# Product of q and decay moved to VectorE, narrowing steps spread evenly, first unit reordered with its constants filled by GpSimd

## The chip, the cores and the metric

The kernel runs on one core of a Trainium2 chip. Five engines work from queues of their own: TensorE (PE, with its weight loads PEld), VectorE (DVE), ScalarE (ACT), GpSimd (POOL) and SyncE (SP, which here only issues transfers). The metric is the device time of one execution in microseconds; the kernel before takes 841.13 us, the median of 3 runs (839.98 to 841.34).

## The reference

Three stages follow one another. Inputs are float32, but the weights of the third stage (`moe2_w_in`, `moe2_w_out`) are float64 and reach the chip as pairs of 32-bit words.

```
f = 1/(1+exp(-f_logit))                        # 4 batches, 8 heads, 768 steps, 48 wide
for t: state = f[t][:,None]*state + outer(k[t],v[t]);  y[t] = q[t] @ state
x = y as (3072, 384);  logits = x @ w_gate     # 8 experts, each takes exactly 384 tokens,
                                               # handed out greedily by logit
x[mask_e] = relu(x[mask_e] @ w1[e]) @ w2[e]
h = x @ w_in;  out = (h*clip(h+3,0,6)/6) @ w_out
```

## The kernel before, in words

`attention` computes the first stage and the logits. The time axis is cut into 24 chunks of 128 steps (index `j`), and two chunks make a unit of 256 steps (12 units, index `u`). All heads are done together. For each unit f, k and q are loaded as pairs of neighbouring steps. `decay` makes ft = (tanh(f/2)) and then 0.5*x+0.5 on ScalarE (L76, L77), and the product of each pair of decays on VectorE into `pmf` (L78). `queries` multiplies the even q by the decay (L85, GpSimd) and copies the odd q (L86, ScalarE). `keys` does the same for k (L81 VectorE, L82 ScalarE). TensorE then transposes: `decays` (L91, ScalarE copies the result to `ff`, L94), `turned` for q and k (L112). VectorE runs a scan for prefix products (`prefix`, L98), a reciprocal (`ends`, L100), a reversed scan (`suffix`, L106), and scales the transposed q and k by them (`scaled`, L125, to `qt` and `kh`). `kept` (L103) stores the decay of a chunk.

For each chunk `ya_mm` issues the state matmuls (L151) and the scores of the next chunk (L145), interleaved; `a_ev` copies the scores out (L177, ScalarE) and masks them (L178, GpSimd); `y_mm` multiplies by v (L202) and ScalarE copies the result to `yt` (L203 or L204); `kt_mm` transposes `kh` (L185, L186); `kv_mm` makes the state's increment (L213), which VectorE adds (L220) and GpSimd scales (L221); `l_mm` gives x and the logits (L227, L229, L232). PSUM tiles named `pT` rotate through five banks, so a transpose may have to wait until an earlier tile of the rotation has been read.

The order is written out by hand in the loop over `j`. With `ti=0` (odd `j`) the unit after the current one is started: `tg(0)` to `tg(3)` call `slot` with n=0 to 3, and with `ti=1` (even `j`) with n=4 to 7. `slot` issues that slot's transposes and its VectorE operations (table `OPS`), and puts a "fill" behind the first of them (or behind the deferred operations of `late`, where the slot has none).

The fill, `take(i)`, advances the generator `prep` by `PREP[ti][i]` steps, and `END[ti]` more are taken at the end of a chunk: the narrowing of the float64 weights. A block of 512 columns takes three steps: (a) ScalarE's rounding copy (L720) and GpSimd's remainder (L721) of the block before, and VectorE's first operation on this block (L923); (b) VectorE L925; (c) VectorE L927, and the transfer (L933) that refills the freed buffer, of which there are two. Blocks of `w_out` (L958, L963 in place of L720, L721) take four. Before, the steps are taken as follows:

```
PREP=((2,0,1,0),(0,0,2,0)); END=(0,1)
```

That is three per chunk up to j=19, then two per slot until none are left. In this order step (c) and the next step (a) fall into the same fill: L720 of a block stands on ScalarE's queue right behind VectorE's L927 of that block.

Ahead of the loop, constants are filled on VectorE (L27 to L59), SyncE issues f, k, q of unit 0 in halves of four heads and then v and the gate's weights (L235 to L239), and the loop at L246 prepares unit 0, one half wholly after the other. Behind the attention come the routing and eight experts.

Of the kernel before, what the change touches and what calls it, by code (L numbers as in the profile page):

```python
# [10 lines left out]
F32=mybir.dt.float32; F32R=mybir.dt.float32r; BF=mybir.dt.bfloat16; I32=mybir.dt.int32; U32=mybir.dt.uint32  # L11
AF=mybir.ActivationFunctionType; OP=mybir.AluOpType; AX=mybir.AxisListType
PS=bass.MemoryType.PSUM
B,H,S,D=4,8,768,48
C=128; U=256; G=C//2; NP=4; NU=B*S//U; NCH=B*S//C
PMIN=2.0**-60; PB=5

def attention(tc, q,k,v,f,wg, x_dram, lg, ident, pmin, ranges, prep, setup, spin):
    nc=tc.nc
    ctx=ExitStack()  # L20
    with ctx:
        ld=ctx.enter_context(tc.tile_pool(name="ald",bufs=2))
        cs=ctx.enter_context(tc.tile_pool(name="acs",bufs=1))
# [4 lines left out]
        for nm in 'kq':  # L28
            t=cs.tile([128,2,NP,2,64],F32,name=f"pm{nm}")
# [3 lines left out]
        ft=cs.tile([128,2,H,D],F32,name="ft")  # L33
        L=G+1; W2=4*L
        held=ps.tile([128,512],F32,name="pC"); m0=held[:,:W2-1]; m1=held[:,512-W2:]
        nc.vector.memset(held,0.0)
        for n in range(4):
            nc.vector.memset(held[:,n*L+G-1:n*L+G],PMIN)
            if n: nc.vector.memset(held[:,n*L-1:n*L],1.0)
        PXB=[]  # L40
        for i in range(2):
            t=cs.tile([128,NP,2,L],F32,name=f"P{i}"); nc.vector.memset(t,1.0); PXB.append(t)
        SW=cs.tile([128,NP,2*D+8],F32,name="sw"); nc.vector.memset(SW,0.0)
        for s in range(2):
            for o in range(2):
                b=(s^o)*D
                nc.vector.tensor_copy(SW[64*s:64*s+48,o::2,b:b+D],ident[64*s:64*s+48,None,64*s:64*s+D].to_broadcast([48,NP//2,D]))
        VP=[]
        for i in range(2):
            t=cs.tile([128,2,H,64],F32,name=f"v{i}"); nc.gpsimd.memset(t[:,:,:,D:],0.0); VP.append(t)  # L50
        KHB=[]
        for i in range(2):
            t=cs.tile([128,NP,U],F32,name=f"kh{i}"); KHB.append(t)
        St=[]
        for i in range(2):
            t=cs.tile([128,NP,64],F32,name=f"St{i}"); nc.vector.memset(t[:,:,D:],0.0); St.append(t)
        FF=[]
        for i in range(2):
            t=cs.tile([128,W2+4],F32,name=f"ff{i}"); nc.vector.memset(t,0.0); FF.append(t)  # L59
        raw={}  # L60
        def load(u,nm,h0=0,h1=H):
            b,o=divmod(u*U,S)
            if nm!='v':
                src={'f':f,'k':k,'q':q}[nm]
                t=ld.tile([128,H,2*D],F32,name=nm+"r",bufs=1) if h0==0 else raw[nm,u]
                nc.sync.dma_start(t[:,h0:h1],bass.AP(tensor=src.tensor,offset=src.offset+b*H*S*D+h0*S*D+o*D,ap=[[2*D,128],[S*D,h1-h0],[1,2*D]]))
            else:
                t=VP[u%2]
                for c in range(2):
                    nc.sync.dma_start(t[:,c,:,:D],bass.AP(tensor=v.tensor,offset=v.offset+b*H*S*D+(o+c*C)*D,ap=[[D,C],[S*D,H],[1,D]]))  # L70
            raw[nm,u]=t
        view=lambda u,nm: raw[nm,u].rearrange("p h (r d) -> p r h d",d=D)
        home=lambda nm,r: perm[nm][:,r].rearrange("p a s d -> p (a s) d")[:,:,:48]
        def decay(u,i,h0=0,h1=H):
            x=ft[:,:,h0:h1]
            if i==0: nc.scalar.activation(x,view(u,'f')[:,:,h0:h1],AF.Tanh,scale=0.5)  # L76
            elif i==1: nc.scalar.activation(x,x,AF.Identity,bias=half[:,0:1],scale=0.5)  # L77
            else: nc.vector.tensor_mul(perm['f'].rearrange("p a s d -> p (a s) d")[:,h0:h1,:48],ft[:,0,h0:h1],ft[:,1,h0:h1])  # L78
        def keys(u,i,h0=0,h1=H):
            x=view(u,'k')[:,:,h0:h1]  # L80
            if i==0: nc.vector.tensor_mul(home('k',0)[:,h0:h1],x[:,0],ft[:,1,h0:h1])  # L81
            else: nc.scalar.copy(home('k',1)[:,h0:h1],x[:,1])  # L82
        def queries(u,i,h0=0,h1=H):
            x=view(u,'q')[:,:,h0:h1]
            if i==0: nc.gpsimd.tensor_tensor(out=home('q',0)[:,h0:h1],in0=x[:,0],in1=ft[:,0,h0:h1],op=OP.mult)  # L85
            else: nc.scalar.copy(home('q',1)[:,h0:h1],x[:,1])  # L86
        KH={};QT={};PC={};PX={};SX={}
        V=nc.vector
        def decays(u,pairs):
            pt=ps.tile([128,512],F32,name="pT",bufs=PB).rearrange("p (a c g) -> p a c g",a=NP,c=2)  # L90
            for p in pairs: nc.tensor.transpose(pt[:,p].rearrange("p c g -> p (c g)"),perm['f'][:,p].rearrange("p a d -> p (a d)"),ident)  # L91
            for h in sorted({p//2 for p in pairs}):
                ff=FF[h][:,:W2].rearrange("p (a c g) -> p a c g",a=2,c=2)
                nc.scalar.copy(ff[:,:,:,1:],pt[:,2*h:2*h+2])  # L94
        flat=lambda t: t.rearrange("p a c g -> p (a c g)")
        def prefix(u,h):
            PX[u]=PXB[u%2]
            V.tensor_tensor_scan(flat(PX[u][:,2*h:2*h+2])[:,1:],FF[h][:,1:W2],m0,1.0,op0=OP.mult,op1=OP.max)  # L98
        def ends(u,h):
            V.reciprocal(m1.rearrange("p (a c g) -> p a c g",a=2,c=2)[:,:,:,G],PX[u][:,2*h:2*h+2,:,G])  # L100
# [3 lines left out]
        def suffix(u,h):  # L104
            SX[u,h]=wk.tile([128,2,2,L],F32,name="S",bufs=2)
            V.tensor_tensor_scan(flat(SX[u,h])[:,1:][:,::-1],FF[h][:,2:W2+1][:,::-1],m1[:,1:][:,::-1],0.0,op0=OP.mult,op1=OP.max)  # L106
        PT={}
        def turned(u,nm,h):
            pt=ps.tile([128,512],F32,name="pT",bufs=PB).rearrange("p (a g r) -> p a g r",a=2,r=2)
            for a in range(2):  # L110
                for r in range(2):
                    nc.tensor.transpose(pt[:,a,:,r],perm[nm][:,r,2*h+a].rearrange("p s d -> p (s d)"),ident)  # L112
            PT[u,nm,h]=pt
        def scaled(u,nm,h):
            if nm=='k': o=KH[u]=KHB[u%2]
            elif h==0: o=QT[u]=wk.tile([128,NP,U],F32,name="qt")
            else: o=QT[u]
            pt=PT.pop((u,nm,h))
            x=SX[u,h] if nm=='k' else PX[u][:,2*h:2*h+2]
            x=x.rearrange("p a c g -> p (a c) g")  # L120
            i0=pt.rearrange("p a (c g) r -> p (a c) g r",c=2); out=o[:,2*h:2*h+2].rearrange("p a (c g r) -> p (a c) g r",c=2,r=2)
            if nm=='k': i1=x[:,:,1:][:,:,:,None].to_broadcast([128,4,G,2])
            else:
                i1=x[:,:,0:G]; i1=bass.AP(tensor=i1.tensor,offset=i1.offset,ap=list(i1.ap)+[[1,2]])
            V.tensor_tensor(out=out,in0=i0,in1=i1,op=OP.mult)  # L125
# [107 lines left out]
            later.append(lambda: nc.sync.dma_start(x_dram[j*C:(j+1)*C,:],y.rearrange("p a d -> p (a d)")))  # L233
        ranges=ranges(lambda: ps.tile([128,384],F32,name="pT",bufs=PB),lambda: ps.tile([128,512],F32,name="pT",bufs=PB))
        for h in (0,4):  # L235
            for nm in 'fkq': load(0,nm,h,h+4)
        load(0,'v')
        for s in range(2):
            for o in range(2): nc.sync.dma_start(SW[64*s:64*s+48,o::2,2*D:],wg.rearrange("(p s d) e -> s d p e",p=NP,s=2)[s^o][:,o::2])  # L239
# [1 line left out]
        def warm(n):  # L241

            t=ps.tile([128,512],F32,name="pT",bufs=PB)
            for _ in range(n): nc.tensor.matmul(t[:,:128],ident,ident,start=True,stop=True)
        warm(WARM[0])
        for h in range(2):  # L246
            hh=(4*h,4*h+4)
            for i in range(3): decay(0,i,*hh)
            for i in range(2): queries(0,i,*hh)
            decays(0,(2*h,2*h+1))  # L250
            for i in range(2): keys(0,i,*hh)
            prefix(0,h); ends(0,h)
            warm(WARM[1])
            turned(0,'q',h); suffix(0,h); scaled(0,'q',h)
            turned(0,'k',h); scaled(0,'k',h)
            warm(WARM[1+h])
        kept(0)
        for nm in 'fqk': load(1,nm)
        later=[]
# [7 lines left out]
        next(prep)  # L267
        while later: later.pop(0)()
        constants,early=setup()
        PREP=((2,0,1,0),(0,0,2,0)); END=(0,1)  # L270
        for j in range(-1,NCH+1):
            tu,ti=divmod(j+1,2)
            tu+=1
            if j>=0 and j%2==0 and j//2+1<NU: load(j//2+1,'v')
            def take(i):
                for _ in range(PREP[ti][i] if j<20 else 2): next(prep,None)
            def tg(i): slot(tu,4*ti+i,(lambda: take(i)) if j>=0 else None)
            if j==NCH: spin(lambda: ps.tile([128,384],F32,name="pT",bufs=PB),TAIL[0])
            tg(0)
            if 0<=j-1<NCH: l_mm(j-1)  # L280
            if j==NCH: spin(lambda: ps.tile([128,384],F32,name="pT",bufs=PB),TAIL[1])
            tg(1)
            while later: later.pop(0)()
            if 0<=j<NCH: y_mm(j,0)
            ya_mm(j)
            if j+1<NCH:
                a_ev(j+1,0)
                a_ev(j+1,1)
            if ti==1: refill(tu+1,'f',2)
            if 0<=j<NCH: y_mm(j,1)  # L290
            if j>=0: kv_mm(j)
            tg(2)
            if ti==0 and tu<NU: kept(tu)
            if ti==0: refill(tu+1,'f',0)
            if j+1<NCH: kt_mm(j+1)
            if ti==1:
                for i in range(2): refill(tu+1,'q',i)
            tg(3)
            if ti==0: refill(tu+1,'f',1)
            if ti==1:  # L300
                for i in range(2): refill(tu+1,'k',i)
            if j>=0: next(constants,None)
            if j>=NCH-4: next(ranges,None)
            if j in (17,22,24): next(early)
            if j<20:
                for _ in range(END[ti] if j>=0 else 0): next(prep,None)
# [843 lines left out]
```

## Time and profile before

| | |
|---|---|
| median of 3 runs | 841.13 us |
| the profiled execution's own time | 845.23 us |
| its span, first to last instruction | 843.2 us |
| PE busy | 793.5 us, 94% |
| PEld busy | 761.9 us, 90% |
| DVE busy | 549.6 us, 65% |
| ACT busy | 364.0 us, 43% |
| POOL busy | 134.7 us, 16% |
| mean granted TensorE clock | 0.982 |

Busy shares are means over stages with different limits. TensorE's row is modelled from pipelined matmuls, so 94% does not say that it runs at its peak. The attention ends, and the last chunk's L202 starts, at 166.62 us of the span; the experts' first matmul starts at 195.35 us.

### The profile page before, as it was taken

What the parts mean: (1) busy time and instruction counts of PE and PEld (TensorE: products, weight loads), DVE (VectorE), ACT (ScalarE), POOL (GpSimd) and SP (SyncE); (2) the same over time, 40 slices, a digit from 0 to 9 for tenths busy, and PEclk for the clock granted to TensorE, in tenths of its full rate; (3) what the DMA queues carried; (4) which work ended last, traced back from release to release, by engine and by line L of the source; (5) the groups of instructions that cost most, each with busy time, mean ns of one, the idle gap of its engine ahead of it and who ended that gap; (6) DMA issues with size and microseconds to landing.
All of it is one profiled execution on the core that took longest, in us unless ns stands there. A gap on an engine that the chain in (4) does not pass through costs nothing.

```text
span 843.2 us, 16692 instructions
## 1 busy us (share of the span) xinstructions
PE 793.5 (94%) x6387; PEld 761.9 (90%) x6387; DVE 549.6 (65%) x1522; ACT 364.0 (43%) x757; POOL 134.7 (16%) x215
## 2 busy tenths in 40 slices
PE   7887899978999999999999999999999999999994
PEld 6776788767989899899999999999999999999994
DVE  7898789777688647846875776667766523642431
ACT  4776677523244325423542454154316423541431
POOL 2665554211001100010101101100200020010001
PEclk9999899988999999999999999999999999999998
DMA  9898897272013112311422232322232321321000
GB/s 220 201 236 203 204 267 185 59 252 87 1 38 113 57 39 59 101 38 57 134 70 77 87 100 82 91 79 83 87 92 83 91 90 57 113 87 47 10 1 32
DMA packets 99032, 84.54 MB, mean 100 GB/s; under 512 B 67328, under 2 KB 86912, under 8 KB 98944
## 3 DMA queue, kind: packets, MB, share of 16 engines
q1 hardware_dynamic: 95872, 73.96, 31.5%
q0 software_dynamic: 3072, 9.44, 3.6%
q8 instruction: 52, 0.85, 0.4%
q14 instruction: 36, 0.29, 0.1%
HBM read 73.94 MB, written 9.44 MB: 99 GB/s over the span
## 4 chain that ended last, share of the span: by engine, by line
PE 57%; issue 10%; DVE 8%; ACT 2%; DMA 2%; POOL 1%; POOLq 0%; SPq 0%; DVEq 0%; ACTq 0%
PE pF L724 9%; PE acc L724 9%; PE pF L725 9%; PE pF L726 9%; PE acc L726 9%; PE acc L725 9%; DMA xg<-x_dram,q_ids 1%; DVE ga L867 1%; DVE hl L870 1%; ACT hh L869 1%; DVE w1l L773 1%; PE pF L811 1%; POOL out_dram L901 1%; DVE q_ge L502 1%; POOL xg L790 1%
## 5 line engine op out<-in xcount | busy, mean ns | idle before, releaser
L724 PE MATMUL acc<-wo,hh 128*128 128x384 f32 x384 | 134.0, 349 | 0.0
L724 PE MATMUL pF<-xh,wih 128*128 128x384 f32 x384 | 131.0, 341 | 0.0
L867 DVE SCALAR_TENSOR_TENSOR ga<-ga,pF 128x384 f32<-128x384 f32 x128 | 70.8, 553 | 92.3 <-ACT ga L866 92.0
L726 PE MATMUL acc<-wo,hh 128*128 128x384 f32 x384 | 129.7, 338 | 0.0
L725 PE MATMUL acc<-wo,hl 128*128 128x384 f32 x384 | 129.5, 337 | 0.0
L725 PE MATMUL pF<-xh,wil 128*128 128x384 f32 x384 | 129.4, 337 | 0.0
L726 PE MATMUL pF<-xl,wih 128*128 128x384 f32 x384 | 129.3, 337 | 0.0
L866 ACT ACTIVATE ga<-pF,three 128x384 f32<-128x384 f32 x128 | 74.1, 579 | 98.9 <-PE pF L726 92.1
L869 ACT CAST hh<-ga 128x384 fp32r<-128x384 f32 x128 | 65.8, 514 | 98.4 <-DVE ga L867 92.9
L870 DVE TENSOR_TENSOR hl<-ga,hh 128x384 fp32r<-128x384 f32 x128 | 71.2, 556 | 29.7 <-ACT hh L869 27.7
L832 ACT ACTIVATE hh<-pF 128x384 fp32r<-128x384 f32 x64 | 31.5, 492 | 132.4 <-PE pF L726 125.1
L901 POOL DMA_INDIRECT out_dram<-ga,q_ids x24 | 24.3, 1011 | 396.7 <-ACT ga L899 393.9
L833 DVE SCALAR_TENSOR_TENSOR hl<-pF,hh 128x384 fp32r<-128x384 f32 x64 | 35.6, 556 | 71.2 <-ACT hh L832 70.8
L724 PEld LDWEIGHTS acc<-wo,hh 128*128 128x128 f32 x384 | 72.5, 189 | 1.6 <-ACT ga L866 1.5
L725 PEld LDWEIGHTS acc<-wo,hl 128*128 128x128 f32 x384 | 72.5, 189 | 0.2 <-DVE hl L870 0.2
L726 PEld LDWEIGHTS acc<-wo,hh 128*128 128x128 f32 x384 | 72.4, 188 | 0.0
L724 PEld LDWEIGHTS pF<-xh,wih 128*128 128x128 f32 x384 | 72.2, 188 | 0.0
L725 PEld LDWEIGHTS pF<-xh,wil 128*128 128x128 f32 x384 | 72.2, 188 | 0.0
L726 PEld LDWEIGHTS pF<-xl,wih 128*128 128x128 f32 x384 | 72.1, 188 | 0.0
L724 PE MATMUL pF<-xh,w1h 128*128 128x384 f32 x192 | 66.8, 348 | 0.6 <-ACT xh L802 0.6
L724 PE MATMUL acc<-hh,w2h 128*128 128x384 f32 x192 | 65.9, 343 | 0.0
L726 PE MATMUL pF<-xl,w1h 128*128 128x384 f32 x192 | 64.9, 338 | 0.0
(285 smaller groups left out, 1623.5 us busy)
## 6 DMA issues: line engine op xcount, KB each, us to landing
wst<-in_moe_w_dram SPq DMA_DIRECT2D x58, 192.0 KB, 2.4
wst<-in_moe_w_dram SPq DMA_DIRECT2D x42, 256.0 KB, 3.0
pw<-in_moe_w_in_dram SPq DMA_DIRECT2D x12, 512.0 KB, 5.1
wo<-in_moe_w_out_dram SPq DMA_DIRECT2D x16, 384.0 KB, 4.3
pm<-in_moe_w_out_dram SPq DMA_DIRECT2D x32, 192.0 KB, 2.5
pm<-in_moe_w_in_dram SPq DMA_DIRECT2D x30, 192.0 KB, 2.6
v<-in_v_dram SPq DMA_DIRECT2D x24, 192.0 KB, 5.2
x_dram<-y SPq DMA_DIRECT2D x24, 192.0 KB, 4.9
```

The source lines that it names most:

```text
L502: V.scalar_tensor_tensor(ge[:,c0:c1],x[:,c0:c1,None].to_broadcast([128,c1-c0,32]),base[:,0:1],grid[:,None,:].to_broadcast([128,c1-c0,32]), ...
L724: nc.tensor.matmul(out, ahi, bhi, start=start, stop=False)
L725: nc.tensor.matmul(out, alo, bhi, start=False, stop=False)
L726: nc.tensor.matmul(out, ahi, blo, start=False, stop=stop)
L773: nc.vector.tensor_tensor(out=lo,in0=got[i],in1=hi.bitcast(F32),op=OP.subtract)
L832: nc.scalar.activation(hh,p,AF.Relu)
L833: s.defer(2,lambda: nc.vector.scalar_tensor_tensor(hl,p,0.0,hh.bitcast(F32),op0=OP.max,op1=OP.subtract))
L866: nc.scalar.activation(a,p,AF.Relu,bias=s.three[:,0:1])
L867: late(f,1,lambda: nc.vector.scalar_tensor_tensor(g,a,6.0,p,op0=OP.min,op1=OP.mult))
L869: late(f,1,lambda: nc.scalar.copy(gh,g))
L870: late(f,3,lambda: nc.vector.tensor_tensor(out=gl,in0=g,in1=gh.bitcast(F32),op=OP.subtract))
L901: st=nc.gpsimd.indirect_dma_start(out=s.out,out_offset=bass.IndirectOffsetOnAxis(ap=ids[:,t:t+1],axis=0),in_=o,in_offset=None)
```

## The change

The narrowing steps are spread: one per slot in three of four slots of every chunk, none at the chunk's end, up to j=20 in place of 19. The product of q and decay goes to VectorE, save for unit 0. For unit 0 the loads come in the order f, q, k, the two halves are interleaved by hand, and most constants are filled by GpSimd, some with fewer instructions or fewer elements.

```
-        for n in range(4):
-            nc.vector.memset(held[:,n*L+G-1:n*L+G],PMIN)
-            if n: nc.vector.memset(held[:,n*L-1:n*L],1.0)
+        every=lambda o,n: held[:,o:o+n*L].rearrange("p (n l) -> p n l",l=L)[:,:,0:1]
+        nc.vector.memset(every(G-1,4),PMIN); nc.vector.memset(every(G,3),1.0)
...
-            t=cs.tile([128,NP,2,L],F32,name=f"P{i}"); nc.vector.memset(t,1.0); PXB.append(t)
-        SW=cs.tile([128,NP,2*D+8],F32,name="sw"); nc.vector.memset(SW,0.0)
-        for s in range(2):
-            for o in range(2):
-                b=(s^o)*D
-                nc.vector.tensor_copy(SW[64*s:64*s+48,o::2,b:b+D],ident[64*s:64*s+48,None,64*s:64*s+D].to_broadcast([48,NP//2,D]))
+            t=cs.tile([128,NP,2,L],F32,name=f"P{i}"); nc.gpsimd.memset(t[:,:,:,0:1],1.0); PXB.append(t)
+        SW=cs.tile([128,NP,2*D+8],F32,name="sw")
...
-            t=cs.tile([128,NP,64],F32,name=f"St{i}"); nc.vector.memset(t[:,:,D:],0.0); St.append(t)
+            t=cs.tile([128,NP,64],F32,name=f"St{i}"); nc.gpsimd.memset(t[:,:,D:],0.0); St.append(t)
...
-            t=cs.tile([128,W2+4],F32,name=f"ff{i}"); nc.vector.memset(t,0.0); FF.append(t)
+            t=cs.tile([128,W2+4],F32,name=f"ff{i}"); nc.gpsimd.memset(t,0.0); FF.append(t)
+        for t in VP: nc.gpsimd.memset(t[:,:,:,D:],0.0)
+        nc.gpsimd.memset(SW,0.0)
+        for s in range(2):
+            for o in range(2):
+                b=(s^o)*D
+                nc.gpsimd.tensor_copy(SW[64*s:64*s+48,o::2,b:b+D],ident[64*s:64*s+48,None,64*s:64*s+D].to_broadcast([48,NP//2,D]))
...
-            if i==0: nc.gpsimd.tensor_tensor(out=home('q',0)[:,h0:h1],in0=x[:,0],in1=ft[:,0,h0:h1],op=OP.mult)
+            if i==0: (nc.vector if u else nc.gpsimd).tensor_tensor(out=home('q',0)[:,h0:h1],in0=x[:,0],in1=ft[:,0,h0:h1],op=OP.mult)
...
-            for nm in 'fkq': load(0,nm,h,h+4)
+            for nm in 'fqk': load(0,nm,h,h+4)
...
-        for h in range(2):
-            hh=(4*h,4*h+4)
-            for i in range(3): decay(0,i,*hh)
-            for i in range(2): queries(0,i,*hh)
-            decays(0,(2*h,2*h+1))
-            for i in range(2): keys(0,i,*hh)
-            prefix(0,h); ends(0,h)
-            warm(WARM[1])
-            turned(0,'q',h); suffix(0,h); scaled(0,'q',h)
-            turned(0,'k',h); scaled(0,'k',h)
-            warm(WARM[1+h])
+        lo,hi=(0,4),(4,8)
+        for i in range(3): decay(0,i,*lo)
+        decays(0,(0,1))
+        for i in range(2): queries(0,i,*lo)
+        keys(0,0,*lo)
+        for i in range(2): decay(0,i,*hi)
+        keys(0,1,*lo)
+        prefix(0,0); ends(0,0); suffix(0,0)
+        warm(WARM[1])
+        turned(0,'q',0)
+        decay(0,2,*hi)
+        decays(0,(2,3))
+        scaled(0,'q',0)
+        turned(0,'k',0)
+        for i in range(2): queries(0,i,*hi)
+        for i in range(2): keys(0,i,*hi)
+        scaled(0,'k',0)
+        prefix(0,1); ends(0,1); suffix(0,1)
+        warm(WARM[1])
+        turned(0,'q',1); scaled(0,'q',1)
+        turned(0,'k',1); scaled(0,'k',1)
+        warm(WARM[2])
...
-        PREP=((2,0,1,0),(0,0,2,0)); END=(0,1)
+        PREP=((1,0,1,1),(1,0,1,1)); END=(0,0)
...
-                for _ in range(PREP[ti][i] if j<20 else 2): next(prep,None)
+                for _ in range(PREP[ti][i] if j<21 else 2): next(prep,None)
```

## Rows read from the trace of the kernel before

**Rows 1.** Busy time by stretch: length; PE, PEld, DVE, ACT, POOL; clock, DMA share, GB/s.
```profile
0.00:20.38 20.38, 14.49 (x135) 13.25 (x135) 15.14 (x46) 9.93 (x21) 4.96 (x13) 1.00 0.90 219
...
39.03:52.25 13.22, 11.05 (x205) 9.92 (x201) 11.70 (x22) 8.77 (x20) 8.52 (x14) 1.00 0.82 211
...
80.45:96.76 16.31, 14.14 (x204) 12.77 (x200) 11.62 (x22) 8.92 (x20) 8.88 (x16) 0.79 0.76 177
...
157.29:166.62 9.33, 8.23 (x155) 7.26 (x152) 4.80 (x20) 5.07 (x12) 3.43 (x6) 1.00 0.12 44
166.62:195.35 28.73, 20.24 (x296) 17.27 (x292) 18.00 (x66) 6.85 (x15) 6.31 (x6) 0.82 0.75 251
195.35:843.18 647.83, 631.58 (x3783) 617.60 (x3783) 392.32 (x1155) 249.40 (x502) 46.74 (x69) 0.99 0.23 68
```

**Rows 2.** Waits from 26.89 to 122.58: total us, times, longest.
```profile
ACT wih L720 <- DVE pm L927: 19.1, 12, 2.6
PE pT L185 <- ACT yt L203: 6.6, 3, 2.4
PE pT L112 <- ACT yt L203: 5.3, 3, 2.5
DVE pm L923 <- DMA pw<-in_moe_w_in_dram: 2.1, 3, 1.0
PE pT L227 <- DVE St L220: 1.8, 2, 1.5
PE pT L227 <- ACT kt L186: 1.4, 1, 1.4
```

**Rows 3.** Timeline of TensorE at one such wait: start, us, instruction, idle before it.
```profile
43.27 0.66 PE L185 MATMUL pT<-ident,kh 128*128 128x128 f32 x4 [2.10 <-ACT yt L203]
```

**Rows 4.** Timeline of ScalarE at the same place.
```profile
40.97 0.62 ACT L720 CAST wih<-pm 128x512 fp32r<-128x512 f32 x1 [2.09 <-DVE pm L927]
```

**Rows 5.** Timeline of VectorE there, and the same operations elsewhere.
```profile
16.38 0.56 DVE L81 TENSOR_TENSOR pmk<-kr,ft 128x384 f32<-128x384 f32 x1 [0.77 <-DMA kr<-in_k_dram]
...
37.55 1.25 DVE L81 TENSOR_TENSOR pmk<-kr,ft 128x384 f32<-128x384 f32 x1
38.72 1.49 DVE L925 SCALAR_TENSOR_TENSOR pm<-pw,pm 128x512 uint32<-128x512 uint32 x1
40.25 0.69 DVE L927 SCALAR_TENSOR_TENSOR pm<-pw,pm 128x512 uint32<-128x512 uint32 x1
...
62.64 0.42 DVE L923 TENSOR_SCALAR pm<-pw 128x512 uint32<-128x512 uint32 x1
...
68.31 1.26 DVE L923 TENSOR_SCALAR pm<-pw 128x512 uint32<-128x512 uint32 x1 [1.02 <-DMA pw<-in_moe_w_in_dram]
...
71.04 0.67 DVE L925 SCALAR_TENSOR_TENSOR pm<-pw,pm 128x512 uint32<-128x512 uint32 x1
```

**Rows 6.** Timeline of GpSimd at the same place.
```profile
37.10 1.28 POOL L721 TENSOR_TENSOR wil<-pm,wih 128x512 fp32r<-128x512 f32 x1 [0.36 <-ACT wih L720]
38.34 1.32 POOL L85 TENSOR_TENSOR pmq<-qr,ft 128x384 f32<-128x384 f32 x1
```

**Rows 7.** Timeline of the start: GpSimd's first fills, then ScalarE and VectorE.
```profile
1.33 0.55 POOL L50 MEMSET v<- 128x256 f32 x2
5.99 0.59 POOL L85 TENSOR_TENSOR pmq<-qr,ft 128x192 f32<-128x192 f32 x1 [4.11 <-DMA qr<-in_q_dram]
...
4.20 0.61 ACT L77 ACTIVATE ft<-ft,half 128x384 f32<-128x384 f32 x1
20.70 0.84 ACT L76 ACTIVATE ft<-fr 128x768 f32<-128x768 f32 x1 [1.50 <-DMA fr<-in_f_logit_dram]
...
5.75 0.56 DVE L59 MEMSET ff<- 128x264 f32 x2
6.35 0.45 DVE L78 TENSOR_TENSOR pmf<-ft 128x192 f32<-128x192 f32 x1
```

**Rows 8.** Busy time of ten microseconds in which the transfers never paused; columns as in rows 1.
```profile
30.00:40.00 10.00, 9.74 (x183) 8.90 (x183) 8.65 (x16) 6.82 (x16) 6.91 (x12) 1.00 1.10 272
```

More of the change, by code (lines that the diff above doesn't have):

```diff
@@ L36, in attention @@
         nc.vector.memset(held,0.0)
-        for n in range(4):
-            nc.vector.memset(held[:,n*L+G-1:n*L+G],PMIN)
-            if n: nc.vector.memset(held[:,n*L-1:n*L],1.0)
+        every=lambda o,n: held[:,o:o+n*L].rearrange("p (n l) -> p n l",l=L)[:,:,0:1]
+        nc.vector.memset(every(G-1,4),PMIN); nc.vector.memset(every(G,3),1.0)
         PXB=[]
         for i in range(2):
-            t=cs.tile([128,NP,2,L],F32,name=f"P{i}"); nc.vector.memset(t,1.0); PXB.append(t)
-        SW=cs.tile([128,NP,2*D+8],F32,name="sw"); nc.vector.memset(SW,0.0)
-        for s in range(2):
-            for o in range(2):
-                b=(s^o)*D
-                nc.vector.tensor_copy(SW[64*s:64*s+48,o::2,b:b+D],ident[64*s:64*s+48,None,64*s:64*s+D].to_broadcast([48,NP//2,D]))
+            t=cs.tile([128,NP,2,L],F32,name=f"P{i}"); nc.gpsimd.memset(t[:,:,:,0:1],1.0); PXB.append(t)
+        SW=cs.tile([128,NP,2*D+8],F32,name="sw")
         VP=[]
         for i in range(2):
-            t=cs.tile([128,2,H,64],F32,name=f"v{i}"); nc.gpsimd.memset(t[:,:,:,D:],0.0); VP.append(t)
+            t=cs.tile([128,2,H,64],F32,name=f"v{i}"); VP.append(t)
         KHB=[]
```

## The prediction, made before the changed kernel was run

> **What bounds the kernel now.** I read the busy time by stretch first, then the waits of the stretch that the change touches, then the timeline of each engine at one such wait. The stretches [rows 1] show two kernels in one. From 195.35 us on TensorE is busy 631.58 of 647.83 us: the experts, which the change doesn't touch. Ahead of that lies the attention, where no engine is full: in 39.03 to 52.25, one pair of chunks, TensorE has 11.05 of 13.22 us and VectorE 11.70. A pair is the loop's natural period (one unit is prepared in it). From 26.89 to 122.58 seven pairs take 95.69 us, 13.67 each.
>
> The waits of these 95.69 us [rows 2] say why. TensorE waits 6.6 + 5.3 us for `yt`, ScalarE's copies that free PSUM banks, and 1.8 + 1.4 us for other releases: 15.1 in all. ScalarE for its part waits 19.1 us, 12 times, for VectorE's L927 ahead of L720. The timelines join the two. ScalarE's L720 starts at 40.97 after 2.09 us idle [rows 4], when L927 (40.25, 0.69 long) has ended [rows 5]; the copies behind L720 on ScalarE's queue free the bank, and TensorE's L185 starts at 43.27 after 2.10 us idle [rows 3]. And L927 is late because VectorE was held: L81 takes 1.25 us beside GpSimd's L721 and L925 takes 1.49 beside GpSimd's L85 [rows 5, 6], where alone they take 0.56 and 0.67 [rows 5]. So the narrowing, which nobody needs yet, blocks ScalarE's queue, and that blocks TensorE.
>
> A second loss follows from the first: the granted clock is 0.79 over 80.45 to 96.76 [rows 1], that is, part of it at 1.2 GHz and the rest at 2.4, and TensorE loses 0.21 x 16.31 = 3.4 us. Without waits and at the full clock a pair would take (95.69 - 15.1 - 3.4)/7 = 11.0 us. That is TensorE's own floor here.
>
> **The narrowing steps.** The count stays at three per chunk, but L927 of a block and L720 of it now lie in different slots: L927 in n=0 or n=4, L720 in n=2 or n=6, behind the copies L177 and L203 on ScalarE's queue. L927 needs only VectorE's turn, and between n=0 and n=2 VectorE has but two scans and some small operations ahead, so ScalarE should find L927 done and the `yt` waits (11.9 us) go. What is late next is VectorE itself or a transfer. The refill of a buffer is issued with L927 and read by the L923 two blocks on: formerly four steps later within one chunk, now four steps that span about one and a half chunks, so the waits of L923 for its transfer (2.1 us [rows 2]) don't grow by that.
>
> **q on VectorE.** GpSimd loses 1.32 us per pair [rows 6]. VectorE gains an instruction of L81's shape, 0.56 us, and loses the hold on L925, 1.49 - 0.67 = 0.82. VectorE's pair goes from 11.70 [rows 1] to 11.70 + 0.56 - 0.82 = 11.44 us. What remains open is L721, 1.28 us twice per pair. It now starts after L203 has been copied out, when VectorE has L925 (n=3) or L923, L85, L925, L81 (n=6, n=7) in its queue. A hold costs 1.25 - 0.56 = 0.69 us as with L81; the pair of the rows holds one such, so none gives 10.75 and two give 12.1 us. With TensorE's floor that bounds a pair to 11.0 and, with a wait of 1 us for a transfer as at 68.31 [rows 5] on top of two holds, 13.0. I take 12.0, near the two-hold case, as VectorE then hands over `kh` late and TensorE waits for it. Seven pairs: 7 x (13.67 - 12.0) = 11.7 us gained (4.7 to 18.7).
>
> **The first unit.** VectorE's fills run until 6.3 us and L78 starts at 6.35, while its input, ScalarE's L77, was ready at 4.81 [rows 7]. With the fills on GpSimd L78 starts about 1.5 us earlier, and the interleaving takes waits for `ff` out of the second half. GpSimd takes some dozen fills and copies; two of 256 elements took 0.55 us [rows 7], so a dozen cost 2 to 5 us and end at 3.5 to 6.5, at worst 0.5 us behind the time when it started unit 0's q (5.99). TensorE turns q only after ScalarE's copy of the odd q, which hides that; without this cover the cost is the same 0.5 us. Loading q ahead of k delays k by one transfer, and L81's product is needed last in a half: nothing. But the gain need not last: ScalarE's tanh at 20.70 waits 1.50 us for unit 2's f, the transfers are at a share of 0.90 over the first 20.38 us [rows 1, 7], and the same bytes must come first in either order; only the issues of k and of the narrowing's blocks move up with the earlier copies. Bounds 0 and 2, and I take 0.8.
>
> **The end.** From 122.58 to 166.62 the loop takes 44.04 us for four pairs, 11.0 each, at TensorE's floor already. Fewer ScalarE waits there, against five steps that move from j=20 to j=21, and two from there into j=22, where VectorE is busy only 4.80 of 9.33 us [rows 1]. I take 0 (from 1.5 gained to 1.5 lost). The 28.73 us of routing at a clock of 0.82 [rows 1] move as a block.
>
> **Sum.** 11.7 + 0.8 + 0 = 12.5 us off the profiled execution's 845.23 (span 843.2 and 2.0 around it) gives 832.7. The median of the runs lies 4.1 us below the profiled execution, which gives 828.6, so 829. If the runs don't have the half-rate stretch (3.4 us), their gain is 9.1 and the time 832. The forecast's own range is 823 to 834.
>
> **Rivals.** (1) The transfers become the bound. In the ten microseconds in which they never paused they moved 272 GB/s at a share of 1.10 [rows 8]; a pair moves 13.22 us x 211 GB/s = 2.79 MB [rows 1], which takes 10.3 us at that rate. That is under 12.0 but close to it, and a mean share of 0.82 [rows 1] leaves room for bursts: one wait of 0.8 us per pair makes 12.8, the gain 7 x 0.87 + 0.8 = 6.9, the time 834. For it: L923 already waits for its blocks. Against: 2.1 us in seven pairs is little. The Trainium skill (DMA: Bandwidth & Descriptors, section Specifications) gives about 358 GB/s for one core from HBM and line rate only from 512 bytes per descriptor; by that figure 2.79 MB would be an estimated 7.8 us and no bound at all. The row's 272 GB/s is what this mix reached, and the measurement decides.
>
> (2) The stall only moves: ScalarE still meets an unfinished L927, one slot later, or TensorE waits as long for `kh` or the state. Then only VectorE's own saving of 0.26 us per pair and a part of the `yt` waits (say a quarter, 3 us) remain: 1.8 + 3 = 5 us, 836. For it: VectorE has 11.4 us of work in a pair, so it has hardly any lead. Against: the L720 waits are placed right behind L927 and nowhere else.
>
> (3) Slower, by held VectorE instructions. If L721 meets two-operand instructions both times (0.8 each, L925's price beside GpSimd), and the masks and the state's scaling on GpSimd hold L923 (1.26 in place of 0.42, so up to 0.8 more [rows 5]) as often, VectorE's pair is 11.44 - 0.69 (the present hold) + 2 x 0.8 + 2 x 0.8 = 13.95 us, and since VectorE would then be the bound with no lead to hide it, the pair takes that: 7 x (13.95 - 13.67) = 2.0 us lost, and with the end's 1.5 lost and the start's gain of 0.8 it is 844. It decides from 3.1 us of holds per pair. For it: every hold in the rows is real, and L85 itself becomes a two-operand VectorE instruction. Against: it needs four full holds in each pair, and GpSimd has 1.32 us less to do. The Trainium skill (GPSIMD Engine Reference, section Key points) says that GpSimd shares its SBUF interfaces with VectorE and collides with VectorE instructions that have two SBUF inputs; by that rule the moved product can be held too. The trace agrees as far as L81's 1.25 against 0.56 us goes.
>
> **Chances.** Forecast 0.60; (1) 0.18; (2) 0.13; (3) 0.09. The range 821 to 838 holds the forecast with its low tail, (1) and most of (2). This kernel's runs can tell 0.2%, or 1.7 us, from no change. Faster: the forecast, nearly all of (1) and most of (2), 0.87. Within 0.2%: 0.05. Slower: 0.08.
>
> **What would show it.** Right: in the trace after, waits of ScalarE's L720 for L927 fall from 19.1 us to under 5, TensorE's waits for `yt` from 11.9 to under 3, the granted clock stays at 1.00 through the loop, a pair takes 11.5 to 12.5 us, and L925 next to the q product takes 0.7 in place of 1.49. L78 of unit 0 starts near 4.9. Wrong: VectorE without idle time and TensorE waiting for `kh` or St (rival 3 or 2), or L923 and L76 waiting for transfers by more than 5 us in the same stretch (rival 1). A time over 838 would mean that the ScalarE stall was not what set the period.

## The result, and the profile after

The changed kernel takes 829.9 us (median of four runs, 826.85 to 832.84) against 841.24 of the kernel before on the same chip: a ratio of 0.9862 with an interval of 0.9821 to 0.9904. The forecast was 829. The profiled execution took 832.84 us with a span of 831.1; like that of the kernel before (845.23 us) it is one of the slower ones.

In the part that the change touches every line of `attention` after the setup is one further down (L220 is L221), and the narrowing's L923, L925, L927 and L720, L721 are L935, L937, L939 and L732, L733. First the busy time by stretch of the kernel after (start:end, length; PE, PEld, DVE, ACT, POOL; clock, DMA share, GB/s), cut at the same instructions as [rows 1]: the seven pairs, two single pairs of them, the last chunk, the routing, the experts.

```profile
27.15:110.47 83.32, 77.78 (x1360) 69.56 (x1356) 80.62 (x162) 63.51 (x142) 48.21 (x75) 1.00 0.98 250
38.55:49.97 11.42, 10.93 (x205) 9.92 (x201) 11.35 (x23) 8.76 (x20) 7.85 (x12) 1.00 0.97 248
49.97:62.88 12.91, 11.02 (x176) 9.32 (x172) 12.84 (x25) 9.44 (x20) 6.71 (x11) 1.00 0.96 253
143.88:152.23 8.35, 8.04 (x155) 7.27 (x152) 7.42 (x25) 5.48 (x13) 3.83 (x6) 1.00 0.14 50
152.23:181.39 29.16, 23.52 (x295) 20.24 (x291) 17.88 (x64) 6.87 (x15) 6.38 (x6) 0.66 0.75 248
181.39:831.10 649.71, 633.24 (x3783) 619.45 (x3783) 392.27 (x1155) 249.40 (x502) 46.69 (x69) 0.99 0.23 68
```

The seven pairs as one stretch of the kernel before:

```profile
26.89:122.58 95.69, 80.42 (x1361) 72.35 (x1357) 81.10 (x154) 63.71 (x143) 55.61 (x82) 0.96 0.87 221
```

The account of the 12.1 us of span, stretch by stretch: the start +0.3 (26.89 to 27.15), the seven pairs -12.4 (95.69 to 83.32), the end of the loop -2.3 (44.04 to 152.23 - 110.47 = 41.76), the routing +0.4 (28.73 to 29.16), the experts +1.9 (647.83 to 649.71). Of the 12.4 us, 2.6 are TensorE's busy time (80.42 to 77.78): the trace before has a piece at the lower clock here (0.96 in the mean), the trace after has none. The pairs are now 11.9 us each, in seven lengths from 10.99 to 13.35, and VectorE is busy in 80.62 of the 83.32 us. Its work is as long as before (81.10); the idle time beside it has gone from 14.6 to 2.7 us. In the pair 38.55:49.97 it is busy 11.35 of 11.42 us. So an engine is full here now, which was not so in any stretch of the loop in [rows 1].

The waits of the same stretch after (total us, times, longest), against [rows 2]:

```profile
DVE St L221 <- PE pT L214: 1.6, 3, 0.8
PE pT L186 <- DVE qt L126: 1.6, 2, 0.9
PE pT L92 <- ACT kt L187: 1.3, 2, 0.7
ACT wih L732 <- DVE pm L939: 1.0, 2, 0.7
PE pT L228 <- DVE St L221: 0.9, 2, 0.5
DVE pm L935 <- DMA wo<-in_moe_w_out_dram: 0.5, 1, 0.5
```

ScalarE's 19.1 us for L927 have become 1.0, TensorE's 11.9 us for `yt` are gone, and TensorE waits 4.9 us in all (15.1 before). By the prediction's own signs this is its mechanism at work. The experiments below say that the time was not gained there. The line that the prediction passed over stood in the same view of the kernel before:

```profile
DVE St L220 <- PE pT L213: 8.4, 5, 4.1
```

There VectorE, the engine with the most work in the stretch, stands idle and waits for TensorE. Four of the five waits are of 0.9 to 1.3 us. The longest, the last line below, is of another kind: over 86.00 to 92.00 the granted clock was 0.50 to 0.52, so TensorE itself ran at 1.2 GHz and was late by that. In e2 below, whose trace has no such piece, the five waits make 6.0 us. Places in the timeline of VectorE before (start, us, instruction, idle before it):

```profile
47.53 0.55 DVE L78 TENSOR_TENSOR pmf<-ft 128x384 f32<-128x384 f32 x1
49.07 0.36 DVE L220 TENSOR_TENSOR St<-St,pT 128x192 f32<-128x192 f32 x1 [0.99 <-PE pT L213]
49.34 0.68 DVE L927 SCALAR_TENSOR_TENSOR pm<-pw,pm 128x512 uint32<-128x512 uint32 x1
49.94 0.73 DVE L923 TENSOR_SCALAR pm<-pw 128x512 uint32<-128x512 uint32 x1
50.60 0.68 DVE L125 TENSOR_TENSOR kh<-pT,S 128x512 f32<-128x512 f32 x1
51.20 1.25 DVE L81 TENSOR_TENSOR pmk<-kr,ft 128x384 f32<-128x384 f32 x1
52.37 1.50 DVE L925 SCALAR_TENSOR_TENSOR pm<-pw,pm 128x512 uint32<-128x512 uint32 x1
...
93.58 0.36 DVE L220 TENSOR_TENSOR St<-St,pT 128x192 f32<-128x192 f32 x1 [4.07 <-PE pT L213]
```

and the place around 49.07 in the kernel after, with the last step that lies ahead of it:

```profile
44.16 0.68 DVE L939 SCALAR_TENSOR_TENSOR pm<-pw,pm 128x512 uint32<-128x512 uint32 x1
...
46.04 0.88 DVE L79 TENSOR_TENSOR pmf<-ft 128x384 f32<-128x384 f32 x1
46.84 0.34 DVE L221 TENSOR_TENSOR St<-St,pT 128x192 f32<-128x192 f32 x1
47.11 0.58 DVE L935 TENSOR_SCALAR pm<-pw 128x512 uint32<-128x512 uint32 x1
47.61 0.86 DVE L86 TENSOR_TENSOR pmq<-qr,ft 128x384 f32<-128x384 f32 x1
48.39 0.68 DVE L126 TENSOR_TENSOR kh<-pT,S 128x512 f32<-128x512 f32 x1
48.99 1.17 DVE L937 SCALAR_TENSOR_TENSOR pm<-pw,pm 128x512 uint32<-128x512 uint32 x1
50.08 0.54 DVE L82 TENSOR_TENSOR pmk<-kr,ft 128x384 f32<-128x384 f32 x1
```

Before, VectorE ran dry ahead of L220, and then had two narrowing steps directly behind it, and a third with L81 and GpSimd's holds behind those. After, the step of n=4 lies ahead of that place (44.16), L221 starts without idle time, and one step less is behind it.

### The profile page after: what moved, and what is told of

It reads as the page before. It is cut to its first block, busy times and chain, and to the rows that moved or that the text cites. A ratio compares the mean times of both kernels' runs of the same rounds, so it can differ in the third digit from the quotient of the medians.

```text
span 831.1 us, 16675 instructions
## 1 busy us (share of the span) xinstructions
PE 794.1 (96%) x6385; PEld 762.7 (92%) x6385; DVE 548.0 (66%) x1517; ACT 364.5 (44%) x757; POOL 125.1 (15%) x215
## 4 chain that ended last, share of the span: by engine, by line
PE 58%; issue 10%; DVE 8%; ACT 2%; DMA 1%; POOL 1%; SPq 0%; POOLq 0%; DVEq 0%; ACTq 0%
PE pF L736 9%; PE acc L736 9%; PE pF L737 9%; PE pF L738 9%; PE acc L738 9%; PE acc L737 9%; DVE ga L879 2%; DVE hl L882 1%; ACT hh L881 1%; DVE w1l L785 1%; ACT ga L878 1%; PE pF L823 1%; POOL out_dram L913 1%; DMA xg<-x_dram,q_ids 1%; PE acc L446 1%
## 5 line engine op out<-in xcount | busy, mean ns | idle before, releaser
L737 PE MATMUL pF<-xh,w1l 128*128 128x384 f32 x192 | 65.3, 340 | 0.0
```

What stands on the lines that cost most here:

```text
L737: nc.tensor.matmul(out, alo, bhi, start=False, stop=False)
```

## The experiments

Below, "the stretch" is always the seven pairs, from the second chunk's L202 or L203 to the same line fourteen chunks later. For each run, look at the stretch's length beside VectorE's busy time and its idle time. For any engine the two add up to the length; what tells the engines apart is which of the two moves when one thing in the kernel is moved.

**The parts alone.** Three kernels of before, each with one part of the change.

```
e1_spread
-        PREP=((2,0,1,0),(0,0,2,0)); END=(0,1)
+        PREP=((1,0,1,1),(1,0,1,1)); END=(0,0)
-                for _ in range(PREP[ti][i] if j<20 else 2): next(prep,None)
+                for _ in range(PREP[ti][i] if j<21 else 2): next(prep,None)
e2_q_vector
-            if i==0: nc.gpsimd.tensor_tensor(out=home('q',0)...
+            if i==0: (nc.vector if u else nc.gpsimd).tensor_tensor(out=home('q',0)...
e3_first_unit
  the fills, the order 'fqk' and the first unit's sequence as in the change, all else as before
```

> The kernel before with the spread of the narrowing steps alone (PREP, END and j<21); q stays on GpSimd and unit 0 as it was. Theory A (ScalarE's queue stands behind L720, which stands behind VectorE's L927; the spread frees it): most of the gain, 7 to 11 us off, 830 to 834; ScalarE's waits for L927 fall from 19.1 us in seven pairs to under 5, TensorE's waits for yt from 11.9 to under 3. Theory B (VectorE is simply too full, and the hold by GpSimd's q product is what counts): 0 to 3 us off, 838 to 841.

> The kernel before with the product of q and decay on VectorE alone. Theory A: L720 still stands right behind L927, so only VectorE's own saving of about 0.26 us per pair shows: 1 to 4 us off, 837 to 840, and TensorE's waits for yt stay above 8 us in seven pairs. Theory B: the hold of 0.82 us on L925 was the cost; 7 us off or more, under 834.

> The kernel before with the edits of the first unit alone (load order, interleaving, fills on GpSimd). Theory A (the transfers set when unit 2's f arrives, so what the start gains is given back by about 27 us): within 1 us of before, 840 to 842, with unit 0's L78 near 4.8 us but the second chunk's L202 at 26.5 to 27.5 us. Rival: the 1.5 us by which L78 comes earlier stay: 839.5 or less.

Against a median of 842.88 us of the kernel before (29 runs): the spread alone 834.38, ratio 0.9905 (0.9871 to 0.9939); q on VectorE alone 840.33, 0.9977 (0.9956 to 0.9997); the first unit alone 842.19, 1.0001 (0.9977 to 1.0025). So most of the gain is the spread's, q's move adds about 2 us, and the first unit's new order is worth nothing that shows. Alone, e1 would have confirmed the prediction: ScalarE's waits for L927 are 2.3 us in it, and none of TensorE's names `yt`. The stretch of e1, then of e2 (its profiled execution has no piece at the lower clock, so that it is 6 us shorter than before, where the runs gain 2):

```profile
27.21:114.99 87.78, 77.63 (x1361) 69.47 (x1357) 84.19 (x155) 63.48 (x142) 56.25 (x82) 1.00 0.95 238
```
```profile
28.09:117.73 89.64, 77.49 (x1360) 69.47 (x1356) 79.30 (x161) 63.33 (x143) 47.29 (x75) 1.00 0.93 237
```

The spread takes VectorE's waits from 13.8 to 3.1 us, but its work grows from 81.10 to 84.19 us, as more of its instructions are held. With q's product on VectorE as well the work is 80.62, although VectorE now does seven products more. The groups show where the 3.6 us went: L925 and L81 (now L937 and L82) are shorter without GpSimd's product of q beside them. Groups of VectorE (instruction xcount | busy, mean ns | idle before), e1:

```profile
L925 DVE SCALAR_TENSOR_TENSOR pm<-pw,pm 128x512 uint32<-128x512 uint32 x11 | 11.4, 1041 | 0.0
L81 DVE TENSOR_TENSOR pmk<-kr,ft 128x384 f32<-128x384 f32 x7 | 7.1, 1011 | 0.0
```

and the kernel after:

```profile
L937 DVE SCALAR_TENSOR_TENSOR pm<-pw,pm 128x512 uint32<-128x512 uint32 x11 | 9.5, 866 | 0.0
L79 DVE TENSOR_TENSOR pmf<-ft 128x384 f32<-128x384 f32 x7 | 5.8, 833 | 0.0
L86 DVE TENSOR_TENSOR pmq<-qr,ft 128x384 f32<-128x384 f32 x7 | 5.4, 773 | 0.0
L82 DVE TENSOR_TENSOR pmk<-kr,ft 128x384 f32<-128x384 f32 x7 | 3.8, 548 | 0.0
```

**The prediction's mechanism alone, in the kernel before.** If ScalarE's L720, queued behind an unfinished L927, were what stops TensorE, handing out L720 one step later must give most of the gain. GpSimd's L721, which reads what L720 writes, moves with it.

```
e4_l720_later (kernel before)
-                split()
-                yield from join(m,got[i])
+                parts=join(m,got[i]); next(parts)
+                yield
+                split()
+                next(parts)
+                yield
+                next(parts,None)
```

> The kernel before in which only the place of L720 and L721 within the narrowing is changed: they come with L925 of the next block, one fill after L927, in place of the same fill. Counts per chunk, q and the first unit are as before. Theory A (it is the place of L720 right behind L927 on ScalarE's queue, and nothing else of the spread): 6 to 10 us off, 831 to 835, ScalarE's waits for L927 under 6 us. Rival (what helps is that VectorE's load is even over the slots): under 2 us off, 839 to 841.

843.72 us, ratio 1.0012 (0.9990 to 1.0034): nothing. Its waits in the stretch:

```profile
PE pT L227 <- ACT kt L186: 4.4, 3, 1.5
...
DVE St L220 <- PE pT L213: 4.2, 4, 1.3
ACT wih L720 <- DVE pm L927: 4.0, 3, 1.7
DVE St L220 <- POOL am L178: 3.5, 1, 3.5
```

ScalarE's wait has gone from 19.1 to 4.0 us and none of TensorE's waits names `yt` any more; TensorE waits 12.3 us in other places, and VectorE waits 11.9 us where it was 13.8. The stall that the prediction wanted to remove was removed, and the time stayed. L721's new place did not eat a gain through holds: VectorE's work is 81.22 us, as before (81.10). And L220 still waits 1.32, 0.97, 0.97 and 0.92 us in four even chunks, as it did before (1.32, 0.99, 1.12, 0.92): so these waits did not come from the `yt` stall.

**The same in reverse, in the kernel after.** L732 and L733 go right behind L939, in the same step.

```
e5_l720_behind (kernel after)
-                split=lambda i=i,m=m,c=c: split_raw(nc,m,wih[:,i//4,c],wil[:,i//4,c],nc.gpsimd)
+                split_raw(nc,m,wih[:,i//4,c],wil[:,i//4,c],nc.gpsimd)
... (and the calls of split that hand them out later fall away)
```

> The changed kernel, but for the 12 blocks of w_in ScalarE's copy (L720) and GpSimd's remainder (L721) are put back right behind VectorE's L927 of the same block, in the same slot; the steps stay evenly spread and q stays on VectorE. Theory A (ScalarE's queue behind L927 is half of the matter, though not all of it, as moving L720 alone gained nothing): a pair gets 1.3 to 2 us longer, 837 to 841, and ScalarE's waits for L927 come back to 10 us or more. Theory C (only VectorE's bunched order mattered): within 2 us of the changed kernel, 828 to 832.

830.06 us, 0.9854 (0.9825 to 0.9883 of 840.95 us for the kernel before beside it, as for e6 to e8), the same as the kernel after. And yet ScalarE waits nearly as long as it did before the change:

```profile
ACT wih L732 <- DVE pm L939: 17.7, 12, 2.5
...
DVE pm L935 <- DMA wo<-in_moe_w_out_dram: 2.5, 1, 2.5
```

TensorE's waits for `yt` come back by only 2.6 us of the 11.9. The two together settle one thing: L720's place right behind L927 is not what costs. 17.7 us of that wait cost nothing under the even spread, and taking it away gives nothing under the bunched order. The reading that fits both is that the wait is a shadow of VectorE's lateness, which reaches TensorE by another way (L186, L229, L220 in e4) when this one is closed.

**One half of the spread at a time.** In e9 a single step of each pair moves from behind L220 (n=6) to n=4, ahead of it. That fills the dry place, and it also takes L927 and L720 apart in the even chunk, which by e4 is worth nothing alone. In e10 only the odd chunk gets the new spread.

```
e9_fill_dry (kernel before)
-        PREP=((2,0,1,0),(0,0,2,0)); END=(0,1)
+        PREP=((2,0,1,0),(1,0,1,0)); END=(0,1)
e10_unload_prefix (kernel before)
-        PREP=((2,0,1,0),(0,0,2,0)); END=(0,1)
+        PREP=((1,0,1,1),(0,0,2,0)); END=(0,1)
```

> The kernel before with one step moved in even chunks: one of the two narrowing steps of slot n=6, behind VectorE's L220 that waits for TensorE's L213, is taken in slot n=4, ahead of it. PREP=((2,0,1,0),(1,0,1,0)), END as before; q on GpSimd. Theory C (VectorE bounds a pair with some 11.5 us of work, and before it stood idle 8.4 us in seven pairs at L220 because the narrowing lay behind that wait): L220's wait falls under 4 us and the time by 3 to 6 us, 836 to 839. Theory A (ScalarE's queue behind L720): L720 and L927 stay together in odd chunks, where the yt wait is, so under 2 us, 840 to 842.

> The kernel before with one step moved in odd chunks: of the two narrowing steps of slot n=0, ahead of the scans of the next unit, one is taken in slot n=2 and L925 goes on to n=3. PREP=((1,0,1,1),(0,0,2,0)), END as before; q on GpSimd. L927 and L720 come apart in odd chunks, and VectorE's way to the scans and to L220 of the odd chunk gets shorter by L923 (0.42 us) at first and L925 later. Theory C: VectorE still stands idle at L220 of even chunks, so a smaller share than the full spread's 8.5 us: 2 to 4 us off, 837 to 839. Theory A: this is the place that stops TensorE, so nearly all of the spread's gain, 6 to 9 us off, 832 to 835.

Against 842.84 us: e9 836.11, 0.9926 (0.9903 to 0.9949); e10 837.53, 0.9945 (0.9924 to 0.9966). By the middle values, one moved step gives about three quarters of what the whole spread gave in e1 (0.74% of 0.95%, with intervals that overlap), with two thirds of the waits that the prediction blamed still there (12.9 of 19.1 us for L927, 7.1 of 11.9 for `yt`). Waits of e9:

```profile
ACT wih L720 <- DVE pm L927: 12.9, 6, 2.9
...
PE pT L112 <- ACT yt L203: 4.6, 4, 1.9
...
DVE St L220 <- PE pT L213: 3.3, 5, 0.7
```

What fell is L220's wait, 8.4 to 3.3 us, and with it all of VectorE's waits, 13.8 to 6.6. Of these 5.1 us, 3.4 are the one long wait at the lower clock; the four others fall from 0.9 to 1.3 us to 0.45 to 0.72 each, so filling that place explains a part of e9's gain and not all of it. E10 brings VectorE's waits to 3.0, but its VectorE work is 85.49 us, the most of all runs (GpSimd still has q): a length of 89.22. By the middle values neither half is the whole spread, but the intervals don't separate them.

**What is left after the change.** Two candidates, the transfers and GpSimd's holds on VectorE, and one edit of where the steps lie. E7 leaves out the transfers of 10 of the 12 blocks of w_in, so its output isn't the reference's; all instructions on the blocks stay. E6 puts the remainders (L733) on VectorE, one step behind ScalarE's copy. E8 takes no narrowing step in chunks 5 and 11, and one more in six later ones.

```
e7_no_loads (kernel after)
+                if i>1:
+                    got[i]=got[i-2]; return
e6_rest_vector (kernel after)
-                yield from join(m,got[i])
+                parts=join(m,got[i]); next(parts)
+                yield
+                rest(); next(parts)
+                yield
+                next(parts,None)
...
+                split=lambda i=i,m=m,c=c: nc.scalar.copy(wih[:,i//4,c],m)
+                rest=lambda i=i,m=m,c=c: nc.vector.tensor_tensor(out=wil[:,i//4,c],...,op=OP.subtract)
e8_pause (kernel after)
-                for _ in range(PREP[ti][i] if j<21 else 2): next(prep,None)
+                for _ in range(0 if j in (5,11) else 1 if i==1 and j in (13,14,15,16,19,20) else PREP[ti][i] if j<21 else 2): next(prep,None)
e11_both_better: the edits of e6 and e8 together;  e12_after_again: the kernel after
```

> The changed kernel without the transfers of 10 of the 12 blocks of w_in: each block reads the buffer of the block two earlier, all else is issued as before. Rival 1 of the prediction (transfers are the next bound): 3 to 7 us off the changed kernel, 823 to 827. Otherwise within 1.5 us of it, 828.5 to 831.5.

> The changed kernel with the remainder of the 12 blocks of w_in on VectorE in place of GpSimd, one step after ScalarE's copy. It takes away GpSimd's two-operand instruction that holds VectorE, and adds about 0.6 us twice per pair to VectorE. If holds are what still costs (some 1.0 us per pair, more in the pairs with the first chunk of a batch): 826 to 830. If VectorE's plain work is the bound and holds are rare: 7 x 0.6 to 1.2 us more, 834 to 838.

> The changed kernel with no narrowing step in chunks 5 and 11 (the pairs that took 12.91 and 13.35 us, where VectorE has no idle time) and one more in chunks 13 to 16, 19 and 20. If VectorE's work and holds make these two pairs long: each 1 to 1.5 us shorter, 827 to 828.5. If something else does (the banks that the missing state update leaves in another rotation): no change, 829 to 831.

> The changed kernel with the remainder of w_in's blocks on VectorE one step later (no holds by GpSimd's L721) and without narrowing steps in chunks 5 and 11, made up for in chunks 13 to 16, 19 and 20. Theory C: a relieved pair only helps where VectorE isn't held right after; without the holds the two pairs' 1.5 us each stay: 825 to 828, below the changed kernel beside it by 2 to 4 us. If VectorE's sum alone counts, moving its steps to other pairs that are near TensorE's floor changes nothing: 828.5 to 831.

> The changed kernel itself, run beside the three others for a direct comparison: 828 to 832.

e7 takes 828.31 us, 0.9844 (0.9810 to 0.9877). Its stretch:

```profile
27.39:112.97 85.58, 80.06 (x1360) 72.32 (x1357) 80.80 (x162) 63.71 (x142) 48.24 (x75) 0.96 0.76 182
```

Its sixth pair, of 15.91 us, has a piece at the lower clock. The first five pairs have a clock of 1.00 in both kernels, and they take 58.21 us at a DMA share of 0.74 where the kernel after takes 58.98 at 0.98. So the transfers set hardly any of the length, though their share of 0.98 looks like it; in the kernel after VectorE waits for them only 0.5 us. E6: 829.05 us, 0.9852 (0.9823 to 0.9881), and a stretch of 83.74 us: no gain over the kernel after that shows, though inside the range expected if holds are what costs, as that range took in the kernel after too. Groups of VectorE in it, columns as above:

```profile
L960 DVE TENSOR_TENSOR wil<-pm,wih 128x512 fp32r<-128x512 f32 x12 | 8.1, 679 | 0.0
L937 DVE SCALAR_TENSOR_TENSOR pm<-pw,pm 128x512 uint32<-128x512 uint32 x11 | 7.7, 702 | 0.0
...
L935 DVE TENSOR_SCALAR pm<-pw 128x512 uint32<-128x512 uint32 x11 | 4.5, 409 | 0.0
```

The twelve remainders are 8.1 us of new work for VectorE, and its busy time only goes from 80.62 to 81.75, because the instructions that GpSimd's L733 held are short again: L935 takes 0.41 us in the mean where it took 0.66 in the kernel after, L937 0.70 where it took 0.87. So these holds cost nearly as much as the work that causes them. E8: 827.29 us, 0.9820 (0.9789 to 0.9851), an interval that overlaps the kernel after's. In its trace the two pairs shrink to 11.0 and 10.2 us, but the pair of chunks 7 and 8, which takes no step more, grows from 11.7 to 13.2, and that of chunks 13 and 14, which does, from 11.0 to 14.2 (2.7 of it a wait for a transfer of `w_out`). E11: 828.26 us (825.33 to 828.91, five runs), 0.9830 (0.9805 to 0.9856), beside e12, the kernel after, at 829.80 (829.38 to 834.48, six runs), 0.9864 (0.9836 to 0.9892). All five runs of e11 lie under all six of e12, but the intervals of the ratios overlap: some 1.5 us, likely and not certain, where 2 to 4 were expected. Its stretch:

```profile
26.45:107.78 81.33, 77.04 (x1361) 69.54 (x1357) 80.78 (x170) 63.16 (x141) 30.99 (x63) 1.00 0.98 250
```

The view lists no wait of VectorE in it, and the length is its work: 80.78 of 81.33 us. A part of the shorter stretch is steps moved behind it, but most of it stays: from its start to the last chunk's L203 e11 takes 123.27 us and e12 124.92. There is no idle time of VectorE left to fill; what would help is less work on VectorE or fewer holds, down to TensorE's 77.0 us. No run here takes work off VectorE.

## Why the prediction came out as it did

**What held.** The time: 829 was forecast, 829.9 measured, and the seven pairs lost 12.4 us where the sum had 11.7. A pair takes 11.9 us, inside the forecast 11.5 to 12.5, the clock in the loop is 1.00, and ScalarE's and TensorE's waits fell as forecast. That VectorE would be what is late next was right too: it is the full engine now. Q's move was put at 0.26 us per pair, 1.8 us in all; alone it measured 2 us, and VectorE's work in e2 is 1.8 us less (81.10 to 79.30). One sign did not come: L925 next to the q product was to take 0.7 us, and as L937 it takes 1.17 there (48.99), beside GpSimd's remainder. A part of the hit is luck: 12.0 was picked between 11.0 and 13.0, the end gained 2.3 us that were not forecast, and the routing and the experts gave 2.3 back. The stated range of 823 to 834 is also narrower than the pairs' own bounds, which off 841.1 us give 822 to 836.

**The step that failed.** "So the narrowing, which nobody needs yet, blocks ScalarE's queue, and that blocks TensorE." Each wait of that chain [rows 2 to 4] is real, but it is not what set the time. E4 cuts the prediction's link and gains nothing, e5 restores ScalarE's wait and loses nothing, e9 leaves the link in the odd chunk, where the `yt` waits are, and gains, by the middle values, three quarters of what the spread is worth. What the runs show in its place is the order of VectorE's own steps: VectorE was idle for 14.6 us of the stretch and is for 2.7 after. A part of the idle time was at L220 in the even chunk (8.4 us, 4.1 of them one wait at the lower clock), with no deferrable step ahead to fill the place, and the bunched steps and the holds came behind it. That L927 was late because of just that idle time fits e4 and e9 but is argued: the three engines wait for one another in a ring, and no run fills that place and changes nothing else. Why 15.1 us of TensorE's waits fell all the same: TensorE's work in the stretch is about as long as VectorE's (80.42 and 81.10 us), so a stretch that loses VectorE's idle time loses TensorE's too, whichever releaser the view names. The number came out because the prediction ran the sum to a bound, VectorE's work plus a hold, and not through the chain: VectorE's work is 11.5 us per pair after, where the sum had 11.44 with one hold and 12.1 with two. It said that a time over 838 would refute the stall; a time under 838 did not show it, since another cause gives the same time.

A second sentence of the prediction fails with it: "A second loss follows from the first", the lower clock from the stall. In e4 no wait of TensorE names `yt`, and the stretch's clock is 0.95; in e2 TensorE waits 8.5 us for `yt`, and the clock is 1.00; in e7 it falls to 0.50 in the pair of 15.91 us, after waits for VectorE and for `kt`. In each of the three falls (before, e4, e7) TensorE had stood idle for part of the few us ahead, but for different releasers. That the loop after runs at 1.00 is what these traces show, and no run ties it to the change.

**The start.** Forecast 0.8 gained, within 0 and 2; measured 0.3 lost in the trace and nothing in e3. L79 of unit 0 does start at 4.81 and not at 6.35, as forecast. The timeline of the start after shows why it is worth nothing, next to [rows 7]:

```profile
4.81 0.36 DVE L79 TENSOR_TENSOR pmf<-ft 128x192 f32<-128x192 f32 x1 [2.31 <-ACT ft L78]
...
20.96 0.84 ACT L77 ACTIVATE ft<-fr 128x768 f32<-128x768 f32 x1 [1.84 <-DMA fr<-in_f_logit_dram]
```

Unit 2's f lands when it did before (20.96 and 20.70 us), and ScalarE waits longer for it, 1.84 us for 1.50. The prediction named this and then took 0.8 of its range; the row it named was the bound.

**The end.** Forecast 0 (within 1.5), measured 2.3 gained. The last chunk takes 8.35 us and not 9.33 [rows 1], with VectorE at 7.42 us for 4.80: the steps moved there fill time that was free. The rest is two of the other three pairs, which are shorter (10.91 to 10.56 and 12.01 to 10.55 us; the third grows from 11.79 to 12.30).

**What gave some back.** The routing ran at a clock of 0.66 (0.82 before) and the experts took 1.9 us more, 2.3 in all. The prediction moved both "as a block". One and the same group of 16 small products, TensorE after:

```profile
158.79 1.87 PE L446 MATMUL acc<-r_before,r_ones 128*128 128x128 bf16 x16
```

and before:

```profile
173.10 1.05 PE L434 MATMUL acc<-r_before,r_ones 128*128 128x128 bf16 x16
```

The granted clock was 0.50 over 158.70 to 160.80 and 1.00 over 173.00 to 174.20, that is 1.2 against 2.4 GHz. By luck it does not matter for the forecast, since the end gained as much.

**The rivals.** (1) The transfers: not the bound by e7. The 10.3 us per pair that the prediction worked out from the 272 GB/s of [rows 8] is no floor either: in the kernel after, the pair 86.13:99.48 moved 286 GB/s. (2) The stall only moves: it did not come with the change, but it is what e4 did. (3) The holds: real and too dear in the forecast. L937 takes a mean of 0.87 us and 1.17 in the place where [rows 5] had 1.49, for 0.67 alone; in pairs that hold the first chunk of a batch, 12.91 and 13.35 us long, L935 took up to 1.27 and L79 up to 1.22. By e6 the holds of GpSimd's remainder that are left are an estimated 8.1 - (81.75 - 80.62) = 7 us in seven pairs, 1 us per pair; rival 3 decides from 3.1. Why those pairs are longer than the others, and why the routing's clock fell, no run here settles.

## What to carry to other kernels

A view of waits names who was late and not why: before a wait is blamed, move the waiting instruction (e4) and put it back (e5), with nothing else than what hangs on it. In a loop where no engine is full, look first for the idle time of the engine with the most work, and for the deferrable instructions on its queue: laid ahead of the place where it runs dry they can fill it, laid behind it they make it later still. Watch its work too, as a new order can raise it by holds (81.10 to 84.19 us in e1). Once one engine's work is the length of the loop, as in e11, order can help only by making that work shorter.

## What the runs showed of the hardware

The times of one kernel go roughly with the mean granted clock: the four runs of the kernel after took 832.84, 830.23, 829.58 and 826.85 us at mean clocks of 0.977, 0.984, 0.983 and 0.988. That is 0.7% between runs of one program, half of what the change gained.

A hold by GpSimd can last longer than one instruction of it, as far as one case shows. In e4 L925 took 3.10 us, for 0.67 alone, beside two of GpSimd's. VectorE's and GpSimd's timelines there:

```profile
52.09 3.10 DVE L925 SCALAR_TENSOR_TENSOR pm<-pw,pm 128x512 uint32<-128x512 uint32 x1
```
```profile
52.21 1.27 POOL L721 TENSOR_TENSOR wil<-pm,wih 128x512 fp32r<-128x512 f32 x1
53.44 1.21 POOL L178 TENSOR_SCALAR_AFFINE_SELECT am<-am 128x512 f32<-128x512 f32 x2
```

L126, a VectorE instruction with one operand in PSUM, was not held here: it took 0.68 us at 48.39 in the timeline after, its usual length, while GpSimd's L733 ran, where L937 right behind it took 1.17.

```profile
48.02 1.59 POOL L733 TENSOR_TENSOR wil<-pm,wih 128x512 fp32r<-128x512 f32 x1
```

The Trainium skill (GPSIMD Engine Reference, section Key points) names two kinds of VectorE instructions that contend with GpSimd: those with two SBUF inputs and those in a 2-port perf mode. The two rows agree with the first kind. L923 and L935 have one tensor in SBUF as input and took 1.26 [rows 5] and 1.27 us for 0.42; by that rule they would be of the second kind, and no trace here names an instruction's perf mode.
